# Threshold attention and a MetaFormer block on one core: moving weight conversion earlier, and spreading the ninth slot's transposes

## The chip, the cores and the metric

The kernel runs on one core of one Trainium2 chip. Its engines are TensorE (PE in the profile, with weight loads as PEld), VectorE (DVE), ScalarE (ACT), GpSimd (POOL) and SyncE (SP), which here only issues transfers. The metric is the device time of one execution in microseconds (us). The kernel before takes 1449.51 us, the median of three runs (1449.02 to 1449.96).

## What is computed

Eight batches of eight heads with 576 tokens and a head dimension of 64 go through an attention that keeps only the scores close to the row's maximum. Its result is then read as 576 rows of 512 features per batch, and goes through a layer norm and two dense layers with a residual.

```python
scores = scale * q @ k.T                       # (8, 8, 576, 576)
scores = where(scores >= max - tau, scores, -1e9)
attn   = exp(scores - max); attn /= attn.sum(-1) + 1e-9
x      = (attn @ v) as (8, 576, 512)           # heads side by side
xn     = (x - mean) / sqrt(var + 1e-6) * g_ln
out    = x + relu(xn @ w_ch1) @ w_ch2          # 512 -> 2048 -> 512
```

`w_ch1` and `w_ch2` arrive in 64 bits, and the kernel turns them into 32-bit numbers itself, with integer operations, while the attention of the first batch already runs.

## The kernel before

The work is cut into 72 **slots**, nine for each batch, numbered here as in the code from n = 0 (the "ninth slot" is n = 8, the "tenth" n = 9). In a slot TensorE makes the scores of two heads for one half of the queries; slot 4 of a batch takes what remains of all heads. The values (attention weights times `v`) of a slot are made in the next slot. Each slot has four **quarters**. What was put aside for a quarter is run at its start, and then some **steps** of the dense layers (the second part) follow; a step is one product of 288 columns.

```python
scores(b, s)
run(n, -1)
rest = exponentials(); es, thr = next(rest)      # max, first two exps
run(n, 0)
conversion.fetch(2)                              # weight chunks: issue the transfer
run_all(stores)
second_part(n, 0)
next(rest, None)                                 # the other two exps
...                                              # turn q, k of the next unit; load_qk
run_all(aside)
tick(1); run(n, 1); second_part(n, 1); tick(2)
den = weights(es, thr, blocks_go)                # threshold, sums, reciprocal
if n <= HP or n == 2 * HP:
    diags = diagonals(den)
run_all(aside); run_all(stores)
if HP < n < SLOTS:
    conversion.fetch(2)
tick(3); run(n, 2); second_part(n, 2)
if HP < n < 2 * HP:
    diags = diagonals(den)
tick(4)
...                                              # turn the attention weights, see below
run_all(aside)
conversion.fetch(2)
tick(5); run(n, 3); ...; second_part(n, 3); tick(6)
run_all(aside)
```

**Weight conversion.** There are 32 chunks of 512 KB (64-bit). Sixteen belong to `w_ch1`, sixteen to `w_ch2`. Rooms of a chunk's size are borrowed from tiles that are not yet in use (`hidden`, `et`, parts of `w2`, one of the `x` tiles, and `stage`). `fetch` issues the transfer of a chunk if a room is free for it. A `tick` moves four chunks one stage on: `end` (ACT, only `w_ch1`), `mask` (DVE), `carry` (POOL) and `begin` (two DVE and two ACT operations that read the raw chunk).

```python
def begin(self):
    ...
    nc.vector.tensor_scalar(out=au, in0=hi, ...)           # L263
    nc.vector.scalar_tensor_tensor(out=au, in0=hi, ...)    # L267
    nc.scalar.activation(words(i)[:, :, 0], ..., AF.Copy)  # L271
    nc.scalar.activation(y, words(i)[:, :, 1], AF.Square)  # L275
def carry(self): nc.gpsimd.tensor_tensor(...)              # L281
def mask(self):  nc.vector.scalar_tensor_tensor(...)       # L290
def end(self):   nc.scalar.mul(dst, made, g)               # L303
```

**Turning the attention weights.** In the first batch (n up to 8) TensorE turns them: each of four blocks is multiplied by a diagonal matrix that holds the reciprocal sums (`tp`, copied by ACT into `em`), then the rest (`tr`). From n = 9 on DVE turns blocks of 32 and a trip through DRAM does the rest (`scr<-et`, then `em<-scr`).

```python
made = turn_weights(s, es, diags)        # yields after block 1 and at the end
at_quarter(n + 1, -1, next, made)
at_quarter(n + 1, 0 if s <= HP else -1, ...next(made)...)
at_quarter(n + 1, 1 if b == 0 and s <= HP else 3, ...values_of(b, s, ...)...)
```

In `values_of`, ACT copies the products from `sc[0]` into `x` (L558). From n = 5 on these products lie in a part of the PSUM tile that holds the scores, so the scores of the next slot wait for that copy.

**Second part.** 129 steps for each of 16 groups (half a batch): 64 into `p1` (first layer, relu on ACT into `hidden`), one for the variance, 64 into `p2`. PSUM tiles of this part share two buffers (`ps_ff`) with `tp`, `tr` and `mean`. `second_part` spreads the steps over the slots until the next group is ready; the group after the first is ready at quarter 43 (slot 10, last quarter).

Of the kernel before, what the change touches and what calls it, by code (L numbers as in the profile page):

```python
# [8 lines left out]
F32 = mybir.dt.float32  # L9
# [3 lines left out]
ALU = mybir.AluOpType  # L13
# [5 lines left out]
def kernel(  # L19
# [31 lines left out]
    nc = tc.nc  # L51
# [4 lines left out]
    HP = H // 2  # L56
    NK = DM // 128
    ND = DF // 128
    J = 4
    NB = S // 32  # L60
    TOK = S // 2
    QH = 256
    SLOTS = 2 * HP + 1
    NG = 2 * B
# [9 lines left out]
    ffn = ctx.enter_context(tc.tile_pool(name="ffn", bufs=2))  # L74
# [8 lines left out]
    ident = consts.tile([128, 128], F32, name="ident")  # L83
# [6 lines left out]
    hidden = consts.tile([128, ND, TOK], F32, name="hidden")  # L90
# [53 lines left out]
    for t in rests + v_rest:  # L144
# [9 lines left out]
        out=scl_sb, in0=tau_sb, scalar1=0.0, scalar2=SCALE, op0=ALU.is_ge, op1=ALU.mult  # L154
# [11 lines left out]
    class Weights:  # L166
# [13 lines left out]
        def __init__(self):  # L180
            self.chunks = [
                (w1_sb[i][:, c : c + WC], w_ch1[i * 128 : (i + 1) * 128, c : c + WC], i)
                for c in range(0, DF, WC)
                for i in range(NK)
            ] + [
                (
                    w2_sb[:, m, d : d + 4].rearrange("p d c -> p (d c)"),
                    w_ch2[d * 128 : (d + 4) * 128, m * 128 : (m + 1) * 128].rearrange(
                        "(d p) c -> p d c", p=128
                    ),  # L190
                    None,
                )
                for m in range(NK)
                for d in range(0, ND, 4)
            ]
            self.n1 = NK * (DF // WC)
            self.fetched = self.begun = self.carried = self.masked = self.ended = 0
            self.raw, self.made, self.due, self.ticks = {}, {}, [], 2
            flat = lambda t: t.rearrange("p a b -> p (a b)")

            x_room = ffn.tile([128, NK, TOK], F32, tag="x", bufs=3, name="x_room")
            stage = consts.tile([128, 8, WC], F32, name="stage")
            et = att.tile([128, NB, 128], F32, tag="et", bufs=1, name="et0")

            n1 = self.n1
            self.free = []
            for t, n, before in (  # L210
                (w2_sb.rearrange("p m d c -> p (m d) c"), ND // 2, lambda p: n1 + 2 * p),
                (hidden, 4, lambda p: 8),
                (et, 2, lambda p: 28),
                (x_room, 1, lambda p: 2 * n1),
                (stage, 4, lambda p: 2 * n1),
            ):
                for p in range(n):
                    self.free.append((before(p), -1, flat(t)[:, p * 2 * WC : (p + 1) * 2 * WC]))
# [192 lines left out]
    def weights(es, thr, divide):  # L411


        den = small.tile([128, 4], F32, tag="den", name="den")
        for i in range(4):
            nc.vector.scalar_tensor_tensor(  # L416
                out=es[:, i], in0=blocks[i], scalar=thr[:, i : i + 1], in1=es[:, i],
                op0=ALU.is_ge, op1=ALU.mult, accum_out=den[:, i : i + 1],
            )
        nc.vector.reciprocal(den, den)  # L420
        for i in range(4 if divide else 0):
            nc.gpsimd.tensor_scalar(  # L422
                out=es[:, i], in0=es[:, i], scalar1=den[:, i : i + 1], scalar2=1.0,
                op0=ALU.mult, op1=ALU.mult,
            )
        return den

    def diagonals(den):

        diags = []  # L430
        for i in range(4):
            if i % 2 == 0:
                two = ffn.tile([128, TOK], F32, tag="o", bufs=6, name="diag")
            diags.append(two[:, i % 2 * 128 : i % 2 * 128 + 128])
            nc.scalar.mul(diags[i], ident, den[:, i : i + 1])
        return diags


# [7 lines left out]
    def turn_weights(s, es, diags):  # L446


        em, er = turned_tiles(s)
        for i in range(4):  # L450
            if i == 2:
                yield
            tp = ps_ff.tile([128, J, 128], F32, tag="ff", name="tp")
            for c in range(J):
                product(
                    tp[:, c], lhsT=es[:, i, c * 128 : (c + 1) * 128], rhs=diags[i],
                    start=True, stop=True,
                )
            if s == HP:
                nc.scalar.copy(  # L460
                    em[:, :, :, 32 * i : 32 * i + 32], tp.rearrange("p c (a x) -> p c a x", a=4)
                )
            else:
                h, j = divmod(i, 2)
                nc.scalar.copy(  # L465
                    em[:, :, 2 * j : 2 * j + 2, 64 * h : 64 * h + 64],
                    tp.rearrange("p c (a x) -> p c a x", a=2),
                )
        tr = ps_ff.tile([64, 4, 128], F32, tag="ff", name="tr")
        for i in range(4):  # L470
            nc.tensor.matmul(
                tr[:, i], lhsT=es[:, i, J * 128 :], rhs=diags[i], start=True, stop=True
            )
        if s == HP:
            nc.scalar.copy(
                er[:64].rearrange("p a (u x) -> p u a x", u=HP),
                tr.rearrange("p u (a x) -> p u a x", a=4),
            )
        else:
            nc.scalar.copy(  # L480
                er[:64].rearrange("p a (h x) -> p h a x", h=2),
                tr.rearrange("p (h j) (a x) -> p h (j a) x", h=2, a=2),
            )
        yield em, er
# [112 lines left out]
    def add_to_x(g, m, p2, rb):  # L597
        o = ffn.tile([128, TOK], F32, tag="o", bufs=6, name="o")
        nc.vector.tensor_mul(o, p2, rb)  # L599
        last = (g, m) == (NG - 1, NK - 1)  # L600
        engine = nc.vector if last else nc.gpsimd
        engine.tensor_tensor(out=o, in0=o, in1=groups[g][:, m], op=ALU.add)  # L602
        aside.append(lambda: store(g, m, o))

    def store(g, m, o):
# [4 lines left out]
    def send(g, m, ot):  # L610
        b, t = divmod(g, 2)
        for i in range(4):
            f = m * 128 + 32 * i
            last = (g, m) == (NG - 1, NK - 1)
            (nc.scalar if last and i % 2 else nc.sync).dma_start(
                out=out[b, t * TOK : (t + 1) * TOK, f : f + 32].rearrange(
                    "(n r) c -> r n c", r=32
                ),
                in_=ot[32 * i : 32 * i + 32].rearrange("p (n c) -> p n c", c=32),
            )  # L620
# [17 lines left out]
    def ffn_steps(g):  # L638
# [5 lines left out]
        for d in range(ND):  # L644
# [12 lines left out]
            if d == 1:  # L657
                sq = ffn.tile([128, NK, TOK], F32, tag="sq", bufs=1, name="sq")
                nc.scalar.activation(sq, xc, func=AF.Square)  # L659
                for c in range(1, NK):  # L660
                    nc.gpsimd.tensor_tensor(out=sq[:, 0], in0=sq[:, 0], in1=sq[:, c], op=ALU.add)  # L661
            if d == 8:
                var = ps_ff.tile([128, TOK], F32, tag="ff", name="var")
                product(var, lhsT=avg_sb, rhs=sq[:, 0], start=True, stop=True)
                rb = ffn.tile([128, TOK], F32, tag="rb", bufs=2, name="rb")
                nc.scalar.activation(sq[:, 1], var, func=AF.Identity, bias=eps_sb)
                aside.append(lambda: root(rb, sq[:, 1], sq[:, 2]))
                yield 1
# [19 lines left out]
    ROOM = (0.6, 1.0, 1.25, 0.35)  # L688
    STEPS = 1 + NK * ND * 2
    queue = []  # L690
    issued = 0
    owed = 0.0
    later_calls = {}

    def at_quarter(n, i, fn, *args):
        later_calls.setdefault((n, i), []).append((fn, args))
# [5 lines left out]
    def ready(g):  # L702

        if g < 2:
            return (24, 43)[g]
        b, t = divmod(g, 2)
        return QUARTERS * (b * SLOTS + (HP, 2 * HP)[t] + 2) + (2, 4)[t]

    def second_part(n, i):

        nonlocal issued, owed
        if not queue:
            return
        at = QUARTERS * n + i
# [40 lines left out]
    load_v(1)  # L755
    for n in range(NS):
        b, s = divmod(n, SLOTS)

        ticks = (1, 3) if n < 6 else range(1, 7)

        def tick(i):
            if i in ticks:
# [20 lines left out]
        second_part(n, 1)  # L783
        tick(2)
        blocks_go = by_blocks(b * HP)
        den = weights(es, thr, blocks_go)
        if n <= HP or n == 2 * HP:
            diags = diagonals(den)
        run_all(aside)
        run_all(stores)  # L790
        if HP < n < SLOTS:
            conversion.fetch(2)
        tick(3)
        run(n, 2)
        second_part(n, 2)
        if HP < n < 2 * HP:
            diags = diagonals(den)
        tick(4)
        box = []
        if blocks_go:  # L800
            scr = turn_blocks(s, es)
            at_quarter(n + 1, 0, lambda s=s, scr=scr, box=box: box.append(fetch(s, scr)))
        else:
            made = turn_weights(s, es, diags)
            at_quarter(n + 1, -1, next, made)
            at_quarter(
                n + 1, 0 if s <= HP else -1, lambda made=made, box=box: box.append(next(made))
            )
        at_quarter(
            n + 1, 1 if b == 0 and s <= HP else 3,  # L810
            lambda b=b, s=s, box=box: values_of(b, s, box[0]),
# [51 lines left out]
```

## Time and profile before

| | value |
|---|---|
| time, median of 3 | 1449.51 us |
| span of the profiled run | 1448.2 us |
| TensorE busy | 1392.3 us (96%) |
| VectorE busy | 871.8 us (60%) |
| ScalarE busy | 421.3 us (29%) |
| GpSimd busy | 437.7 us (30%) |
| mean granted TensorE clock | 0.992 |

The profile also shows the span cut into 40 slices of 36.2 us, with each engine's busy share in tenths. Waits are listed as "engine line <- what ended the wait". A busy TensorE is one whose matmuls are pipelined, so its share is not a share of peak. The starts of the slots can be read from the first matmul of line L384 (scores): slot 3 starts at 46.24 us, slot 6 at 81.48, slot 8 at 132.64, slot 9 at 156.74 and slot 10 at 193.26.

### The profile page before, as it was taken

The page shows a single profiled execution, that of the slowest core. Times are in us where ns is not written, and L with a number is a line of the kernel's source. Part 1 is how long each engine was busy: PE and PEld are TensorE (multiplying, and loading weights), DVE is VectorE, ACT ScalarE, POOL GpSimd, SP SyncE. Part 2 cuts the span into 40 slices and gives each one's busy share as a digit, 9 for nine tenths or more (in the row PEclk, how much of TensorE's full clock was granted, in tenths as well). Part 3 has the DMA queues.
Part 4 walks back from the last instruction along what each step waited for, and adds up shares of the span by engine and source line. Part 5 has one row for each costly group of instructions (what it writes and reads, how often), then busy time and mean ns, then how long its engine had stood idle before and what let it go on. Part 6 is the DMA issues. An engine that isn't in the chain of part 4 may idle for free.

```text
span 1448.2 us, 29660 instructions
## 1 busy us (share of the span) xinstructions
PE 1392.3 (96%) x12168; PEld 855.2 (59%) x12168; DVE 871.8 (60%) x1493; ACT 421.3 (29%) x818; POOL 437.7 (30%) x680
## 2 busy tenths in 40 slices
PE   4889869999999999999999999999999999999998
PEld 3666645655556555565556556565655655565565
DVE  5989756566655566656665565656665566655211
ACT  3887313132221313222131222223131222313020
POOL 2344423233323233232333233232332323223100
PEclk8999989999999999999999999999999999999999
DMA  9613366558755677555865577555775568555301
GB/s 226 166 55 101 60 149 159 141 135 165 183 146 144 156 173 154 162 143 134 189 160 149 136 173 167 148 144 143 180 171 141 140 167 174 152 143 136 78 6 17
DMA packets 466840, 205.12 MB, mean 142 GB/s; under 512 B 275024, under 2 KB 428368, under 8 KB 466704
## 3 DMA queue, kind: packets, MB, share of 16 engines
q1 hardware_dynamic: 461328, 202.57, 57.9%
q8 instruction: 95, 1.56, 0.5%
q10 hardware_dynamic: 5344, 0.66, 0.4%
q14 instruction: 41, 0.34, 0.1%
q0 software_dynamic: 32, 0.00, 0.0%
HBM read 119.41 MB, written 83.76 MB: 140 GB/s over the span
## 4 chain that ended last, share of the span: by engine, by line
PE 87%; DVE 7%; ACT 2%; issue 1%; DMA 1%; POOL 1%; SPq 0%; POOLq 0%; ACTq 0%; DVEq 0%
PE p L100 64%; PE sc L384 10%; PE sc L541 10%; DVE e L416 2%; DVE neg L398 1%; PE tp L100 1%; ACT e L409 1%; DVE w L290 1%; PE mean L100 1%; DVE w L263 0%; DMA em<-scr 0%; DMA stage<-in_moe_w_ch_dram 0%; POOL e L422 0%; PE var L100 0%; ACT em L465 0%
## 5 line engine op out<-in xcount | busy, mean ns | idle before, releaser
L100 PE MATMUL p<-xc,w 128*64 128x288 f32 x4096 | 515.9, 408 | 8.0 <-ACT hidden L655 7.4
L100 PE MATMUL p<-hidden,w 128*64 128x288 f32 x4096 | 513.9, 407 | 0.0
L100 PEld LDWEIGHTS p<-xc,w 128*64 128x64 f32 x4096 | 292.3, 137 | 216.2 <-ACT hidden L655 17.2
L100 PEld LDWEIGHTS p<-hidden,w 128*64 128x64 f32 x4096 | 295.3, 137 | 199.6 <-issue 9.7
L398 DVE TENSOR_REDUCE neg<-sc 128x2 f32<-128x1152 f32 x144 | 188.8, 1353 | 254.2 <-PE sc L384 254.2
L409 ACT ACTIVATE e<-sc,neg 128x576 f32<-128x576 f32 x288 | 194.4, 741 | 259.6 <-DVE neg L398 259.6
L422 POOL TENSOR_SCALAR e<-e,den 128x576 f32<-128x576 f32 x252 | 188.2, 764 | 232.2 <-DVE den L420 232.2
L416 DVE SCALAR_TENSOR_TENSOR e<-sc,thr,e 128x576 f32<-128x576 f32 x288 | 219.3, 812 | 20.5 <-ACT e L409 20.5
L497 DVE STREAM_TRANSPOSE et<-e 128x1152 f32<-128x1152 f32 x112 | 153.3, 1374 | 77.2 <-POOL e L422 54.1
L655 ACT ACTIVATE hidden<-p 128x288 f32<-128x288 f32 x256 | 105.5, 412 | 275.7 <-PE p L100 274.0
L384 PE MATMUL sc<-kT,qT 64*128 64x384 f32 (+3 forms) x1024 | 154.0, 433 | 32.5 <-ACT x L558 12.4
L384 PEld LDWEIGHTS sc<-kT,qT 64*128 64x128 f32 x1024 | 96.2, 194 | 91.0 <-issue 27.8
L402 POOL TENSOR_SCALAR thr<-neg,low_sb 128x2 f32<-128x2 f32 x144 | 41.5, 288 | 356.2 <-DVE neg L398 350.3
L541 PE MATMUL sc<-em,v_in 128*64 128x256 f32 (+1 forms) x1408 | 130.8, 329 | 0.6 <-DMA em<-scr 0.4
L558 ACT COPY x<-sc 128x256 f32<-128x256 f32 x60 | 22.3, 372 | 316.9 <-PE sc L541 293.7
L541 PEld LDWEIGHTS sc<-em,v_in 128*64 128x64 f32 x1408 | 86.1, 137 | 39.3 <-DVE et L497 1.5
L602 POOL TENSOR_TENSOR o<-o,x 128x288 f32<-128x288 f32 x63 | 50.6, 803 | 149.3 <-DVE o L599 149.3
L599 DVE TENSOR_TENSOR o<-p,rb 128x288 f32<-128x288 f32 x64 | 28.1, 439 | 106.4 <-PE p L100 105.8
L567 POOL TENSOR_TENSOR sum<-sum,x 128x256 f32<-128x256 f32 (+1 forms) x64 | 32.4, 506 | 80.8 <-ACT x L558 78.2
L661 POOL TENSOR_TENSOR sq<-sq 128x288 f32<-128x288 f32 x48 | 38.7, 807 | 43.7 <-ACT sq L659 41.2
L567 POOL TENSOR_TENSOR sum<-x 128x256 f32<-128x256 f32 (+1 forms) x32 | 16.8, 525 | 102.8 <-ACT x L558 59.1
L541 PE MATMUL sc<-rest,v_rest 128*64 128x256 f32 (+1 forms) x352 | 44.3, 329 | 0.0
(133 smaller groups left out, 717.9 us busy)
## 6 DMA issues: line engine op xcount, KB each, us to landing
scr<-et SPq DMA_DIRECT2D x252, 288.0 KB, 4.6
em<-scr SPq DMA_DIRECT2D x63, 1024.0 KB, 5.9
out_dram<-ot SPq DMA_DIRECT2D x254, 36.0 KB, 4.2
q_in<-in_q_dram SPq DMA_DIRECT2D x124, 72.0 KB, 3.2
k_in<-in_k_dram SPq DMA_DIRECT2D x120, 72.0 KB, 2.8
v_in<-in_v_dram SPq DMA_DIRECT2D x64, 128.0 KB, 4.4
rest<-scr SPq DMA_DIRECT2D x63, 128.0 KB, 5.9
w<-in_moe_w_ch_dram SPq DMA_DIRECT2D x11, 512.0 KB, 5.4
```

What stands on the lines that cost most here:

```text
L100: nc.tensor.matmul(out[r], lhsT=lhsT[:, r], rhs=rhs, **flags)
L384: nc.tensor.matmul(sc[h][64 * i : 64 * i + 64 if s == HP else 128, at : at + n], lhsT=ql[r] if s == HP else qT[r, half, j * 128 : (j + 1) ...
L398: nc.vector.tensor_reduce(out=neg[:, i], in_=pairs[h], axis=AXL.X, op=ALU.max, negate=True,)
L402: nc.gpsimd.tensor_scalar(out=thr[:, i], in0=neg[:, i], scalar1=-1.0, scalar2=low_sb, op0=ALU.mult, op1=ALU.add,)
L409: nc.scalar.activation(es[:, i], blocks[i], func=AF.Exp, bias=neg[:, i : i + 1])
L416: nc.vector.scalar_tensor_tensor(out=es[:, i], in0=blocks[i], scalar=thr[:, i : i + 1], in1=es[:, i], op0=ALU.is_ge, op1=ALU.mult, accum_o ...
L422: nc.gpsimd.tensor_scalar(out=es[:, i], in0=es[:, i], scalar1=den[:, i : i + 1], scalar2=1.0, op0=ALU.mult, op1=ALU.mult,)
L497: nc.vector.transpose(et[:, :, 64 * h : 64 * h + 64].rearrange("p n (j c) -> p j n c", j=2), es[:, 2 * h : 2 * h + 2].rearrange("p j (n c) ...
L541: nc.tensor.matmul(dst[64 * h : 64 * h + 64], lhsT=vt[:, c, h, :] if c < J else vr[:, h, :], rhs=pick(em[:, c] if c < J else er, hp, h), s ...
L567: nc.gpsimd.tensor_tensor(out=sums[g][:, cols], in0=x[:, 0, cols] if c == 1 else sums[g][:, cols], in1=x[:, c, cols], op=ALU.add,)
L602: engine.tensor_tensor(out=o, in0=o, in1=groups[g][:, m], op=ALU.add)
L655: nc.scalar.activation(hidden[:, d], p1, func=AF.Relu)
```

## The change

It moves the conversion of the weights forward: slots 3 to 5 get a third tick. The extra `fetch` in the middle of slots 5 to 8 is gone, and two kinds of rooms may be borrowed for longer (`hidden` up to chunk 10, `et` up to chunk 32). The diagonals are always made right behind the reciprocal. The four blocks of the ninth slot are turned in four places of the tenth slot (before the quarters, and in quarters 0, 1 and 2) in place of all at its start. The second group of the dense layers is ready one quarter earlier. The variance's product is not made in a slot's first quarter (unless the first layer ends there). The very last addition goes to GpSimd like all others, and the last four stores are all issued by SyncE.

```diff
-                (hidden, 4, lambda p: 8),
-                (et, 2, lambda p: 28),
+                (hidden, 4, lambda p: 10),
+                (et, 2, lambda p: 2 * n1),
... weights(): the diagonals are made here, behind the reciprocal
-    def diagonals(den):
+            if not divide:
+                ...
+                nc.scalar.mul(diags[i], ident, den[:, i : i + 1])
+                continue
... turn_weights()
-            if i == 2:
+            if i:
                 yield
... add_to_x(), send()
-        last = (g, m) == (NG - 1, NK - 1)
-        engine = nc.vector if last else nc.gpsimd
-        engine.tensor_tensor(out=o, in0=o, in1=groups[g][:, m], op=ALU.add)
+        nc.gpsimd.tensor_tensor(out=o, in0=o, in1=groups[g][:, m], op=ALU.add)
-            (nc.scalar if last and i % 2 else nc.sync).dma_start(
+            nc.sync.dma_start(
... ffn_steps()
-            if d == 8:
+            if d >= 8 and rb is None and (part or d == ND - 1):
... ready()
-            return (24, 43)[g]
+            return (24, 42)[g]
... the loop over slots
-        ticks = (1, 3) if n < 6 else range(1, 7)
+        ticks = (1, 3, 4)[: 2 + n // 3] if n < 6 else range(1, 7)
-        if HP < n < SLOTS:
-            conversion.fetch(2)
-            at_quarter(n + 1, -1, next, made)
-            at_quarter(
-                n + 1, 0 if s <= HP else -1, lambda made=made, box=box: box.append(next(made))
-            )
+            for i, at in enumerate(
+                (-1, -1, 0, 0) if s <= HP else (-1, -1, -1, -1) if s < 2 * HP else (-1, 0, 1, 2)
+            ):
+                if i < 3:
+                    at_quarter(n + 1, at, next, made)
+                else:
+                    at_quarter(n + 1, at, lambda made=made, box=box: box.append(next(made)))
```

More of the change, by code (lines that the diff above doesn't have):

```diff
@@ L420, in weights @@
         nc.vector.reciprocal(den, den)
-        for i in range(4 if divide else 0):
+        diags = []
+        for i in range(4):
+            if not divide:
+                if i % 2 == 0:
+                    two = ffn.tile([128, TOK], F32, tag="o", bufs=6, name="diag")
+                diags.append(two[:, i % 2 * 128 : i % 2 * 128 + 128])
+                nc.scalar.mul(diags[i], ident, den[:, i : i + 1])
+                continue
             nc.gpsimd.tensor_scalar(
@@ L425, in weights @@
             )
-        return den
-    def diagonals(den):
[L430 to L435, printed above, removed]
         return diags
@@ L613, in send @@
             f = m * 128 + 32 * i
-            last = (g, m) == (NG - 1, NK - 1)
-            (nc.scalar if last and i % 2 else nc.sync).dma_start(
+            nc.sync.dma_start(
                 out=out[b, t * TOK : (t + 1) * TOK, f : f + 32].rearrange(
@@ L690 @@
     queue = []
-    issued = 0
+    issued = part = 0
     owed = 0.0
@@ L709, in second_part @@
     def second_part(n, i):
-        nonlocal issued, owed
+        nonlocal issued, owed, part
+        part = i
         if not queue:
@@ L785 @@
         blocks_go = by_blocks(b * HP)
-        den = weights(es, thr, blocks_go)
-        if n <= HP or n == 2 * HP:
-            diags = diagonals(den)
+        diags = weights(es, thr, blocks_go)
         run_all(aside)
         run_all(stores)
-        if HP < n < SLOTS:
-            conversion.fetch(2)
         tick(3)
@@ L795 @@
         second_part(n, 2)
-        if HP < n < 2 * HP:
-            diags = diagonals(den)
         tick(4)
```

## The prediction

> **What bounds the kernel now.** I read the page's slices first. They show where TensorE is not full.
>
> ```profile
> PE   4889869999999999999999999999999999999998
> DVE  5989756566655566656665565656665566655211
> PEclk8999989999999999999999999999999999999999
> ```
>
> From slice 8 on (253 us) TensorE stands at 9: nothing but fewer matmuls helps there, and the change removes none. The loss lies in the first seven slices, with VectorE at 9 in slices 3 and 4, and in the sixth, where the clock dips too. So I cut this stretch by slots, at the starts of the score matmuls (from, width, then busy us with counts for PE, PEld, DVE, ACT, POOL, then clock, DMA share and GB/s):
>
> ```profile
> 46.24:57.89 11.65, 10.09 (x109) 7.86 (x109) 11.55 (x18) 10.52 (x22) 5.03 (x5) 1.00 0.94 225
> 57.89:69.66 11.77, 9.99 (x124) 7.47 (x124) 11.67 (x18) 10.41 (x21) 4.83 (x5) 1.00 0.29 92
> 69.66:81.48 11.82, 10.41 (x168) 8.62 (x168) 11.72 (x18) 10.39 (x21) 4.83 (x5) 1.00 0.02 3
> 81.48:109.77 28.29, 24.51 (x228) 15.58 (x224) 22.31 (x37) 22.89 (x47) 14.90 (x17) 1.00 0.28 82
> 109.77:132.64 22.87, 21.36 (x211) 14.14 (x209) 22.46 (x35) 18.25 (x37) 9.63 (x8) 1.00 0.49 144
> 132.64:156.74 24.10, 21.59 (x212) 14.41 (x212) 23.36 (x39) 15.23 (x30) 9.73 (x10) 1.00 0.28 59
> 156.74:193.26 36.52, 24.01 (x212) 19.71 (x212) 18.94 (x31) 8.12 (x14) 11.86 (x13) 0.88 0.40 90
> 193.26:216.41 23.15, 21.20 (x154) 13.41 (x154) 17.34 (x30) 4.24 (x7) 9.67 (x12) 0.89 0.51 117
> ```
>
> These are slots 3 to 10. In slots 3 to 5 VectorE is busy 99% of the time: it bounds them. Slot 9 takes 36.52 us for as many matmuls (212) as slot 8 runs in 24.10. Its waits name the cause; the timelines of PE, ACT and SP show it:
>
> ```profile
> 193.26 4.21 PE L384 MATMUL sc<-kT,qT 64*128 64x384 f32 x16 [9.77 <-ACT x L558]
> 191.70 0.68 ACT L271 ACTIVATE stage<-stage 128x512 int32<-128x512 uint32 x1 [18.66 <-DMA stage<-in_moe_w_ch_dram]
> 192.83 0.38 ACT L558 COPY x<-sc 128x256 f32<-128x256 f32 x1
> 181.33 4.20 SPq L503 DMA_DIRECT2D scr<-et  x4
> 185.63 2.86 SPq L243 DMA_DIRECT2D stage<-in_moe_w_ch_dram  x2
> ```
>
> Slot 10's scores wait 9.77 us for a copy of 0.38 us. The copy stands on ACT behind a `begin` whose chunk was fetched in the same quarter. That fetch stood on SP behind slot 9's four `scr` writes.
>
> **What the Trainium skill says.** "TensorE: Matmul & The Clock Gate", on the array's architecture, says that the ACT and DVE queues are strictly first in, first out. The trace agrees: the copy starts at 192.83, straight behind the two `begin` operations, though its product was ready about 10 us earlier. Part 1 of that page says that an idle TensorE falls to a slower clock. Here the granted clock is 0.88 in slot 9, and the scores after the gap take 4.21 us where those at 216.34 take 2.21. "SBUF — State Buffer", on who interferes with whom, says that some DVE operations and GpSimd exclude each other on a shared port pair. The trace fits: L263 takes 0.41 us, but 1.52 us in cases where a `carry` runs beside it.
>
> **The change part by part.** I stepped through the code's counters (fetch, tick, rooms, steps owed) for both versions; for the kernel before they give the order of transfers and steps in the trace.
>
> *Step unit.* The chain has "PE p L100 x100" in 12.28 us; a step is four such records, 0.49 us. A slot without turning blocks needs 2.14 (scores) + 2.16 (values), with turning 3.73 (`tp`) + 0.90 (`tr`) more: 8.9 us beside the steps.
>
> *Third tick, slots 3 to 5.* The counters put the last three fetches (chunks 29, 30, 31) at the ends of slot 8 (29, 30) and the start of slot 9 (31), where before 29 came at the start and 30, 31 at the end of slot 9. A tick costs VectorE a mask, L263 and L267: from the groups of 46 to 82 us 0.85 + 0.88 + 1.43 = 3.2 us, about 2.7 back to back. VectorE has no gap in slots 3 and 4: 2 x 2.7 = **+5.4 us** on the end of slot 5. The third one, in slot 5, comes behind what slot 6's scores wait for, and slot 6 has gaps on VectorE: +0.5.
>
> *More steps early.* With its group ready a quarter earlier, the pacing puts 32, 25, 29, 29, 30 steps in slots 6 to 10 (before: 28, 25, 26, 26, 28), and 129 in slots 11 to 15 (before 141). The sum is the same; what counts is whether the 12 moved steps (5.9 us) fall in gaps. Slot 6: 28.29 us now, 23.3 of it needed; four more steps +1.5. Slot 7: no change of steps. Slot 8: needs 14.2 + 8.9 = 23.1, and I allow 1.0 for waits: 24.1, as before.
>
> *Diagonals earlier, slots 5 to 7.* ACT then waits for `den` ahead of the relus of quarter 2. In slot 7 `den` is there at 123.5 while PE reaches that quarter at about 122; with two `p1` buffers I put +0.7 on this.
>
> *The stall itself.* In slot 8 nothing is written to `scr` (TensorE turns there), so SP reaches chunk 29 behind the q and k loads: 143.93 + 4.1 us, 15.4 us into the slot. These chunks took 6.0 us to land at this stage (median between 140 and 220 us), so 21.8 us into the slot. ACT comes free at 20.4 (diagonals end at 153.07). The `begin` (1.1) and the copy would end near 23.4, while PE has work until 23.1. So the stall shrinks from 9.77 us to below 1, and chunk 31 lands long before slot 9's first tick.
>
> *Blocks of the ninth slot spread.* PE's waits on ACT in slot 9 are 3 x 0.7 before `tp` and 0.7 before `tr`. Between steps the copies have time, so 2.1 go; the last stays, since `tr` still follows the fourth block. A new wait of about 1.3 is likely: the fourth block needs the buffer of a `p2` that VectorE reads only behind slot 9's thresholds. Slot 9: 14.2 + 8.9 = 23.1 needed, + 2.9 for waits = **26.0, before 36.52**.
>
> *Slot 10.* 30 steps 14.7 + mean 0.6 + 4.3 = 19.6, + 0.6 for a wait = 20.2, before 23.15 (cold scores and a wait of 1.95 for `mean`). *Slots 11 to 15*: -12 steps = -5.9, and -0.7 for the variance of the second group, whose product moves from slot 12's second quarter to slot 11's last. Later groups of the kernel before make it in quarters 1 or 2 already, so four waits of 0.70 stay.
>
> *Tail.* The last addition: 0.80 + handoffs on POOL (1427.67 to 1429.04, 1.37 us from product to transpose) for 0.99 on DVE: +0.4. Four issues on SP take 1.83, two on each of two engines 0.89: +0.9.
>
> | part | us |
> |---|---|
> | third ticks (5.4 + 0.5) | +5.9 |
> | slot 6, steps | +1.5 |
> | slot 7, diagonals | +0.7 |
> | slot 8 | 0.0 |
> | slot 9 (26.0 - 36.5) | -10.5 |
> | slot 10 (20.2 - 23.15) | -3.0 |
> | slots 11 to 15 | -6.6 |
> | tail | +1.3 |
> | sum | -10.7 |
>
> 1449.5 - 10.7 = 1438.8; I say **1438.5 us**.
>
> **The rivals.** *The stall only moves.* Chunk 29 is begun by the tick that follows its fetch, as chunk 30 was before. If SP is late in slot 8, or the q and k loads (small packets, just ahead of it) slow the transfer, ACT blocks there, up to 5 us, with a cold clock behind it. For it: the same code pattern. Against it: no `scr` writes ahead, and a full slot of PE work. It would make 1443 to 1447. *VectorE pays it all.* But for slot 6 (79%), slots 3 to 8 run VectorE at 97 to 99%; if the third ticks collide with `carry` each time (3.2 us) and slots 6 to 8 pass every delay on, about +5 more: 1444. *The early slots swallow the ticks.* The same chunks then leave slots 8 and 9, where VectorE was late (slot 8 at 97%); if slots 7 and 8 also become shorter, -4 more: 1434. *PE was full anyway*, so that only the gap counts: gains of slot 9 alone less the ticks, 1444.
>
> **Range and chances.** The rivals lie between 1434 and 1447, the sum at 1438.8. 1431 to 1447 should hold it 8 times in 10. Over 2% faster would be below 1420.5, which is 18 us beyond the sum; over 2% slower, above 1478.5, would need a stall larger than any in the trace. So faster 0.02, same 0.97, slower 0.01.
>
> **What would show it.** Slots 3 and 4 last 14.3 us; slot 6 starts near 87, slot 9 near 165, slot 10 near 191, slot 11 near 211. The wait of scores for ACT's copy is below 2 us everywhere. The chunk fetches of slot 8 are issued about 15 us into it. No `tp` wait of 0.7 comes three in a row in slot 9. The last DMA issue ends 1.3 us later behind the last matmul. I am wrong if VectorE passes less or more than 2.7 us a tick on to slot 6, or if slot 8's copy waits for a transfer.

## The result, and the profile after

The changed kernel takes 1440.17 us (median of six runs, 1438.01 to 1441.93). Six runs of the kernel before, taken beside them, have a median of 1450.35 us. The ratio is 0.9923, with a 95% interval of 0.9903 to 0.9943: 0.8% faster. Predicted were 1438.5 us, between 1431 and 1447, and "within 2%".

First the slices of the page after. Slice 5 no longer shows an 8, and the 6 in slice 6 has become a 9; slice 3 has gone from 8 to 7. The dip of the clock there is gone as well.

```profile
PE   4879999999999999999999999999999999999998
DVE  5997957556665666566665565656665666655111
PEclk8999999999999999999999999999999999999999
```

Now slots 3 to 10, cut as for the kernel before (from, width, then busy us with counts for PE, PEld, DVE, ACT, POOL; clock, DMA share, GB/s):

```profile
46.38:57.60 11.22, 10.05 (x109) 7.86 (x109) 11.12 (x18) 9.22 (x19) 4.37 (x5) 1.00 0.93 210
57.60:72.06 14.46, 10.13 (x125) 7.47 (x124) 14.32 (x21) 12.31 (x25) 6.36 (x6) 1.00 0.42 137
72.06:86.66 14.60, 10.54 (x168) 8.62 (x168) 14.46 (x21) 11.96 (x24) 6.37 (x6) 1.00 0.22 71
86.66:120.81 34.15, 28.14 (x244) 17.40 (x241) 26.36 (x44) 25.12 (x51) 18.72 (x19) 0.95 0.26 81
120.81:143.09 22.28, 21.63 (x211) 13.95 (x209) 19.62 (x30) 16.41 (x33) 8.82 (x8) 1.00 0.25 72
143.09:166.04 22.95, 22.95 (x227) 15.35 (x225) 22.24 (x38) 14.05 (x27) 9.21 (x10) 1.00 0.44 98
166.04:190.73 24.69, 23.32 (x227) 17.86 (x225) 16.93 (x28) 7.08 (x13) 10.95 (x13) 1.00 0.43 89
190.73:211.18 20.45, 19.70 (x162) 11.58 (x161) 12.59 (x24) 5.30 (x9) 7.80 (x12) 1.00 0.63 144
```

Slot 9 fell from 36.52 to 24.69 us with 15 more matmuls in it. Slots 4 and 5 are 2.7 and 2.8 us longer, with VectorE at 99% as before, and slot 6 is 5.9 us longer. The timelines of SP, ACT and PE at the end of slot 8 show what became of the chunk that used to stall:

```profile
159.01 0.44 SPq L243 DMA_DIRECT2D w<-in_moe_w_ch_dram  x1
163.29 0.70 ACT L271 ACTIVATE w<-w 128x512 int32<-128x512 uint32 x1 [0.59 <-DMA w<-in_moe_w_ch_dram]
164.45 0.39 ACT L555 COPY x<-sc 128x256 f32<-128x256 f32 x1
166.04 2.21 PE L384 MATMUL sc<-kT,qT 64*128 64x384 f32 x16
```

Chunk 29 is issued 15.9 us into slot 8, and ACT waits 0.59 us for it. The copy then starts 1.6 us before the scores, which have no wait. The same ordering hazard is in the code, but TensorE has work over it.

### The profile page after: what moved, and what is told of

The parts are those of the page before. It is cut to its first block, busy times and chain, and to the rows that moved or that the text cites. A ratio compares the mean times of both kernels' runs of the same rounds, so it can differ in the third digit from the quotient of the medians.

```text
span 1438.0 us, 29661 instructions
## 1 busy us (share of the span) xinstructions
PE 1389.3 (97%) x12168; PEld 851.0 (59%) x12168; DVE 868.9 (60%) x1492; ACT 421.7 (29%) x818; POOL 439.0 (31%) x681
## 4 chain that ended last, share of the span: by engine, by line
PE 89%; DVE 5%; ACT 2%; DMA 2%; issue 1%; SPq 1%; POOL 0%; POOLq 0%; DVEq 0%; ACTq 0%
PE p L100 67%; PE sc L538 10%; PE sc L384 10%; DVE e L416 1%; PE tp L100 1%; DMA v_in<-in_v_dram 1%; DVE neg L398 1%; SPq L115 1%; ACT e L409 1%; PE mean L100 0%; DVE et L494 0%; DVE w L263 0%; PE var L100 0%; DMA qk_room<-in_q_dram 0%; ACT hidden L649 0%
## 5 line engine op out<-in xcount | busy, mean ns | idle before, releaser
L384 PE MATMUL sc<-kT,qT 64*128 64x384 f32 (+3 forms) x1024 | 150.0, 424 | 20.9 <-DVE e L416 10.8
```

The source lines that it names most:

```text
L384: nc.tensor.matmul(sc[h][64 * i : 64 * i + 64 if s == HP else 128, at : at + n], lhsT=ql[r] if s == HP else qT[r, half, j * 128 : (j + 1) ...
```

## The experiments

Theory 1: the gain is the stall of slot 9 that goes, since the last chunks are issued ahead of slot 9's `scr` writes; the third ticks and the early diagonals are its price. The rivals were that earlier steps, spread blocks or early conversion as such carry it. "At slot 16" below means the start of slot 16's scores; from there on TensorE is the bound in all these kernels, and they differ by single waits. From slot 16 to slot 71 the traces take between 1021.4 and 1026.1 us (the changed kernel 1022.6, and 1023.8 in its second trace, run 9). Slot starts already differ by up to 1 us at slot 3 between runs of the same kernel. Both limit what such a difference can tell.

**1. The stall alone.** The kernel before, with one more fetch:

```diff
         second_part(n, 1)
         tick(2)
+        if n == SLOTS:                  # slot 9
+            conversion.fetch(2)
```

> The kernel before with one more fetch of two chunks in slot 9, behind its second tick, so that chunks 30 and 31 are issued ahead of slot 9's scr writes. Nothing else of the change. Theory 1 (the change's gain is the stall in slot 9 that goes, less what the third ticks cost): the 9.8 us wait of slot 10's scores for ACT's copy falls below 1 us, slot 9 lasts 25 to 27 us (36.5 before), slot 10 about 21, and the kernel takes 1436 to 1439, ratio 0.990 to 0.993, as good as the changed one without any third tick. Theory 2 (the gain comes from the 12 steps that are done earlier, and from the spread blocks): 1446 or more, since neither is in it.

Measured: 1440.88 us, ratio 0.9911 (0.9878 to 0.9944), against the changed kernel's 0.9923. On SP the two chunks now stand ahead of the `scr` writes, and slot 10's scores start at once:

```profile
169.65 1.80 SPq L243 DMA_DIRECT2D stage<-in_moe_w_ch_dram  x2
183.51 3.81 SPq L503 DMA_DIRECT2D scr<-et  x4
...
183.81 2.21 PE L384 MATMUL sc<-kT,qT 64*128 64x384 f32 x16
```

Slot 9 lasts 26.68 us and slot 16 starts 10.1 us earlier than before. This one fetch gives the whole gain of the change, so theory 1 stands. The ratio is in the range that I expected. The time is 2 to 5 us above it, but the kernel before, measured beside it, took 1453.5 us here. Slot 10 lasted 22.46 us in place of about 21, because the mean still waited 2.03 us for VectorE.

**2. The third tick alone.** The kernel before with `ticks = (1, 3, 4)[: 2 + n // 3]`.

> The kernel before with only the third tick in slots 3 to 5. By the counters chunk 31 is still fetched at the end of slot 9, behind the scr writes, and begun at once. Theory 1: the stall stays at 7 to 10 us, slot 6 starts 5.2 us later, and the kernel gets slower: 1452 to 1456. Rival (converting earlier is what gains, whatever the last fetch does): 1440 to 1444.

Measured: 1451.96 us, ratio 0.9994 (0.9982 to 1.0005): neither slower nor faster. The stall is there as theory 1 says, 7.50 us:

```profile
186.17 1.60 SPq L243 DMA_DIRECT2D stage<-in_moe_w_ch_dram  x1
192.70 0.67 ACT L271 ACTIVATE stage<-stage 128x512 int32<-128x512 uint32 x1 [17.57 <-DMA stage<-in_moe_w_ch_dram]
...
194.27 4.21 PE L384 MATMUL sc<-kT,qT 64*128 64x384 f32 x16 [7.50 <-ACT x L558]
```

But the price came back: slot 6 starts 6.4 us later than before (0.6 of that is there at slot 2 already), and slot 16 only 0.8 later. Slots 7 and 8 are 0.65 and 1.44 us shorter, slot 9 3.9. The scores at the start of slot 9 waited 2.52 us for ACT's copy in the kernel before, and ran slowly behind that:

```profile
156.74 3.73 PE L384 MATMUL sc<-kT,qT 64*128 64x384 f32 x16 [2.52 <-ACT x L558]
```

Here they wait 0.94 us and take 2.21. Of slot 9's 3.9 us, 2.3 are the shorter stall and 1.5 these scores. So I had booked the ticks as pure cost, and most of it comes back as shorter waits later.

**3. The diagonals.** The changed kernel with the diagonals of slots 5 to 7 behind the steps of quarter 2, as before.

> The changed kernel with the diagonals of slots 5 to 7 made where they were before, behind the steps of quarter 2. Slot 6 lasts 34.15 us in the changed kernel, 28.29 before; PE waits 2.77 us there for a relu behind the diagonals, and its matmuls then come at 0.24 us in place of 0.12 for about 3.5 us. Theory 1 (the diagonals are the cause of both): that wait falls to about 1.6, no slow stretch behind it, slot 6 lasts 31 to 31.5, the kernel 1437 to 1438. Rival (the four more steps and the third tick of slot 5 are the cause): slot 6 stays above 33, the kernel at 1440.

Measured: 1438.10 us, ratio 0.9898 (0.9873 to 0.9923), slot 6 at 30.86 us. PE's timeline in slot 6 of the changed kernel:

```profile
106.06 2.16 PE L100 MATMUL p<-xc,w 128*64 128x288 f32 x16 [1.01 <-ACT hidden L649]
110.99 4.18 PE L100 MATMUL p<-xc,w 128*64 128x288 f32 x20 [2.77 <-ACT hidden L649]
```

and with late diagonals:

```profile
106.38 2.16 PE L100 MATMUL p<-xc,w 128*64 128x288 f32 x16 [1.00 <-ACT hidden L652]
110.16 2.65 PE L100 MATMUL p<-xc,w 128*64 128x288 f32 x20 [1.61 <-ACT hidden L652]
```

The wait is 1.2 us shorter, the length of the four diagonals on ACT, and the same 20 matmuls behind it take 2.65 us in place of 4.18. Slot 6 is 3.3 us shorter: 1.2 from the wait, 1.7 from the slow matmuls behind it (1.5 here, 0.2 in the values), 0.4 from a shorter wait of `tp`. Half pace behind this wait is not certain, though: of the five traces in which it lasts 2.76 or 2.77 us, four show it, and run 7 does not (last section).

**4. Two ticks and the extra fetch, in the changed kernel.**

> The changed kernel with two ticks in slots 3 to 5 as before, and the extra fetch of the first run in slot 9. The rest of the change stays. Theory 1: the third ticks are pure cost once the last chunks are fetched ahead of the scr writes; slot 6 starts 5 us earlier than in the changed kernel, slot 9's stall stays away, and the kernel takes 1434 to 1437. Rival (earlier conversion relieves VectorE in slots 7 to 9 by as much as it costs): 1439 to 1441.

With two ticks the rooms in `hidden`, kept to chunk 10 here, are overwritten by relus before one chunk has left them, so one weight chunk is not what it should be; the operations and their order are the same as otherwise. Measured: 1440.81 us, ratio 0.9927. Slot 6 starts 5.6 us earlier, but slot 9 lasts 31.03 us, 6.3 more than in the changed kernel, because the fourth block waits 3.28 us for a buffer that VectorE has to read, and the matmuls behind it run at half pace for a while. By time the rival is right. Run 11 repeats it with sound rooms.

**5. The ninth slot's blocks at the start.** The changed kernel with `(-1, -1, -1, -1)` for all slots above the fourth.

> The changed kernel with all four blocks of the ninth slot turned at the start of slot 9, as before. Slot 9 lasts 24.69 us in the changed kernel, with two waits of 0.7 for ACT's copies. Theory 1 (spreading saves what the waits show): two more waits of 0.7, slot 9 at 26.0 to 26.5, the kernel 1441 to 1442. Rival (the title's change is what removes the stall): the wait of slot 10's scores returns, slot 9 above 30, 1446 or more.

Measured: 1441.69 us, ratio 0.9936 (0.9919 to 0.9954); slot 9 lasts 26.50 us, with all four waits of about 0.7 for ACT's copies. Slot 16 starts 1.5 us later. Spreading these blocks is worth 1.5 to 1.8 us here and has nothing to do with the stall.

**6. The second group ready at quarter 43.**

> The changed kernel with the second group ready at quarter 43 as before, so that slots 6 to 10 get 133 steps in place of 145. Theory 1 (the moved steps fall in few gaps): slot 6 lasts 32 to 33 us in place of 34.15, slots 11 to 15 are 6 us longer together, the wait of the mean for VectorE in slot 10 (1.95 us before) returns; at slot 16 the difference to the changed kernel is +1 to +3 us. Rival (the earlier steps are a main part of the gain): +6 us.

Measured: 1443.51 us, ratio 0.9948 (0.9931 to 0.9965). Slot 6 lasts 32.20 us. At slot 10 this kernel is 5.1 us ahead of the changed one, and at slot 16 0.2 behind (0.5 ahead at slot 6 already, so 0.7 lost): the moved steps are paid where they go, and the small rest is the mean's wait, 1.44 us, and one of 0.70 for a relu in slot 12. Against the trace of run 9, where the changed kernel has no long wait in slot 12, 1.7 us are lost. At slot 71 this kernel is 3.15 us behind. Behind slot 16 it has four waits of 0.70, in the places where the kernel before has them, and the changed kernel has one: 2.1 us. The rest are waits of the values for transfers, which differ from run to run. One of the four in its PE timeline:

```profile
396.88 8.47 PE L100 MATMUL p<-xc,w 128*64 128x288 f32 x68 [0.70 <-ACT hidden L649]
```

**7. The variance as before** (`if d == 8`).

> The changed kernel with the variance's product always behind the ninth block of the first layer, as before. By the counters it moves only for the last group (slot 75, after the attention has ended). Expected: slot starts up to slot 71 within 0.5 us of the changed kernel's up to what runs differ by (0.6 us in the first three slots), time 1438 to 1442. Rival (the variance's place carries part of the gain): waits of PE for ACT's relu of 0.7 us come back in several groups, 3 us or more in the sum.

Measured: 1439.33 us in one run; slot 71 starts 0.4 us earlier than in the changed kernel, and no wait came back. (Slot 6 starts 1.1 us later, ahead of anything that the edit touches.) The variance's rule does nothing that can be seen here. The four waits belong to the ready quarter of run 6: the rounding of steps owed is carried on from group to group, and with 42 in place of 43 the first quarter of slot 21 gets eight steps in place of four (32 matmuls in place of 16 between slot 21's scores and the variance's product in the two traces). The relu that was late in run 6 stands on ACT between the slot's exponentials.

**8. Late diagonals and the old tail**, in the changed kernel.

> The changed kernel with the diagonals of slots 5 to 7 at their old place and the last addition and the last stores as before (VectorE; SyncE and ScalarE in turn). Expected from its parts: the late diagonals took the span from 1438.0 to 1436.6, and the tail behind the last matmul is 6.3 us in the changed kernel, 5.05 before: 1.2 less, a span of 1435 to 1436 and 1436 to 1437.5 us, ratio 0.988 to 0.990; faster than both kernels. Rival (the tail is hidden by the last transfer anyway): no change against the run with late diagonals alone, 1438.

Measured: 1433.82 us, ratio 0.9890 (0.9871 to 0.9909), span 1431.8. The tail behind the last matmul is 5.1 us again, 1.1 less than the changed kernel's 6.2 with GpSimd and SyncE alone. That is what the old tail can give. The medians of runs 3 and 8 lie 4.3 us apart, but they were not taken side by side; their ratios differ by 0.0008, which is 1.2 us. Their operations are the same up to the tail, and yet at slot 71 this profile is 3.7 us ahead of run 3's.

**9 and 10. The changed kernel and that of run 8, side by side.**

> The changed kernel as it is, to stand beside the next run on the same chip. Expected: 1438 to 1441 us, ratio 0.991 to 0.994, slot starts within 1 us of its first profile.

> The kernel of the eighth run once more (changed kernel, diagonals of slots 5 to 7 late, old tail), beside the changed one on the same chip. Expected: 4 to 6 us below it (3.3 from slot 6, 1.2 from the tail), 1433 to 1436 us. Rival (the 1433.8 was a good draw): less than 3 us below.

Measured: 1439.28 us (1437.65 to 1440.60; ratio 0.9911, 0.9895 to 0.9927) and 1436.62 us (1433.46 to 1438.60; 0.9893, 0.9875 to 0.9911). The medians lie 2.7 us apart, which is what the rival said (less than 3). In the traces slot 16 starts 2.7 us earlier and slot 71 5.0, and the spans are 1437.8 and 1431.7; but the second trace is of the fastest of its five runs. So the version is faster than the kernel before; it was below the changed kernel both times, but by how much is left open by the spread of the runs.

**11. Two ticks, the extra fetch, and the rooms to chunk 8**, in the kernel of run 8.

> That kernel with two ticks in slots 3 to 5 as before, the extra fetch in slot 9, and the hidden rooms kept to chunk 8 (the fourth run kept them longer, so one weight chunk was overwritten there). Theory 1 (third ticks are a price of 5 us): slot 6 starts 5.2 us earlier and most of it stays: 1429 to 1431. Theory 3 (VectorE's work is only moved: what slots 4 and 5 lose, slots 7 to 9 gain): slot 6 starts 5.2 us earlier, slots 7 to 9 are 4 to 6 us longer together, with VectorE late in slot 9 and a wait of the fourth block for a buffer that VectorE reads, and the time is 1433 to 1436.

Measured: 1436.26 us, ratio 0.9892 (0.9874 to 0.9909), the same as run 10. Slot 6 starts 5.7 us earlier, slot 10 0.9 later than in run 10. The lead goes in slot 9, which lasts 31.30 us in place of 24.69; slots 7 and 8 took only 0.6 of it. PE's timeline there:

```profile
173.53 1.98 PE L100 MATMUL tp<-diag,e 128*64 128x128 f32 x16 [3.57 <-DVE o L599]
176.19 1.75 PE L471 MATMUL tr<-diag,e 128*64 128x128 f32 x7 [0.69 <-ACT em L465]
```

Without the third ticks VectorE has conversions left in slot 9, reads `p2` late, and the fourth block waits for that buffer; the matmuls behind that wait run at half pace. Theory 3 is right in the sum (the time is just above its range) and theory 1's account of the ticks is wrong: with the blocks spread, they buy back in slot 9 what they cost in slots 4 and 5. Whether they would with the blocks at the start stays open. Run 1 has two ticks and its blocks there, and its slot 9 lasts 26.68 us with three steps fewer; that would leave about 3 us of the lead (an estimate from these two slots), and no run combines it with the rest of run 11.

## Why the prediction was right, point by point

| step | predicted | measured |
|---|---|---|
| start of slot 6 | +5.4 | +5.2 |
| slot 6 | +2.0 | +5.9 |
| slot 7 | +0.7 | -0.6 |
| slot 8 | 0.0 | -1.2 |
| slot 9 | -10.5 | -11.8 |
| slot 10 | -3.0 | -2.6 |
| slots 11 to 15 | -6.6 | -5.5 |
| slot 16 to the last matmul | 0 | -0.7 |
| tail | +1.3 | +1.2 |
| sum (span) | -10.7 | -10.2 |

- **The stall** was read rightly: it went, and the remaining wait of ACT for the transfer was 0.59 us. Run 1 shows that nothing else is needed for it. The rival that it would only move did not come true. By the prediction's own sign, "if slot 8's copy waits for a transfer", it was not quite right: the copy stood behind that `begin`, only too briefly to matter. The 15.4 and 6.0 us that it adds up make 21.4, not 21.8; the `begin` started 20.2 us into the slot.
- **The third ticks** cost 5.2 us ahead of slot 6, at the rate I had taken from the groups. I put them one slot too early: the scores of slot 4 come ahead of slot 3's third tick on VectorE, so slots 4 and 5 grew, not 3 and 4. And the sum has no line for what they relieve later. The third rival, that slots 7 and 8 become shorter, was partly true: they became 1.7 us shorter where I had 0.7 longer. In slot 7 a wait of 1.35 us for a relu is gone, and one of 0.63 for another operation of ACT came. In slot 8 the wait of 2.52 us at its end, which the sum does not name, is gone, against three more steps (1.5). (VectorE stands at 9 in slices 2 and 4 of the page before, and at 8 in slice 3; the prediction has slices 3 and 4.)
- **Slot 6** is the term that was mis-sized. I put 0.5 for the tick, 1.5 for the steps, and the diagonals' price on slot 7. In the traces the 5.9 us are: four more steps 2.0; `tp` waiting 1.0 longer for ACT, 0.6 of it by the third tick of slot 5 (run 2 has this alone) and 0.4 by the diagonals; the relu waiting 1.2 longer behind the diagonals; and 1.7 of half pace behind that wait (1.5 in the 20 matmuls, 0.2 in the values). Run 3 takes the last two away, with 0.4 of the `tp` wait, and gets 3.3 us. In slot 7 the diagonals cost nothing that I can see.
- **Slot 9** came out 1.3 us better than the sum, because the fourth block did not wait for `p2`. Of the 2.9 us for waits the prediction names 0.7 and 1.3; measured are two of 0.69 and 0.68. Runs 4 and 11 show that this wait is real, and larger than I put it, once VectorE is later.
- **The four waits of 0.70** did not stay: after 300 us PE waits for a relu once. The step that failed is "later groups make it in quarters 1 or 2 already": the quarter was right, but not the number of steps ahead of it in the slot. Runs 6 and 7 put this on the ready quarter. In the trace after, 1.8 us of other waits (values for VectorE, at 739 and 907 us) stand against it.
- **Slots 11 to 15** gave 5.5 us in this profile, with a wait of 0.82 us for VectorE in slot 12. In run 9's profile of the same kernel they give the predicted 6.6.
- **Moved steps** are worth 0.7 to 1.7 us up to slot 16 by run 6: paid where they go for the most part.

In short, the main mechanism was right: the stall goes, and the third ticks cost about 5 us ahead of slot 6. That the total came out within 2 us is luck: slot 6 was too low by 3.9 and slots 7 to 9 too high by 3.8.

## What to carry to other kernels

Look at what stands ahead of a transfer in its issuing queue, not only at when the code asks for it: one fetch moved ahead of a write that waits for late data was worth 10 us here, and the rest of the change about nothing. An in-order engine (ACT here) that first reads a fresh transfer and then frees a buffer hands that transfer's latency on to everyone who waits for the buffer. A cost on a busy engine is not a loss until one has looked at where the same work would have stood otherwise.

## What the runs showed of the hardware

A wait of TensorE can cost more than itself: behind some waits the matmuls run at half pace for a while. Take the second wait for a relu in slot 6. Where it lasts 1.59 to 1.61 us (seven traces: the kernel before, runs 1 to 3, 8, 10 and 11), the matmuls behind it keep their pace. Where it lasts 2.76 or 2.77 us, they fall to half of it in four traces of five (the changed kernel, runs 5, 6 and 9). Behind the waits of 3.28 and 3.57 us in slot 9 (runs 4 and 11) 16 `tp` matmuls took 1.98 us in place of 1.09. Behind the wait of 2.77 in the changed kernel the matmuls came every 0.24 us in place of 0.12, for some 3.5 us, and the clock in the profile's window from 113 to 116 us is 0.61:

```profile
113.00:116.00 3.00, 3.00 (x18) 1.64 (x16) 2.93 (x6) 1.74 (x4) 0.06 (x2) 0.61 0.04 10
```

The fifth trace is that of run 7, whose operations up to there are the same. The same 20 matmuls behind the same wait take 2.65 us there in place of 4.18, and a `tp` wait 19 us earlier has half pace behind it instead (in the changed kernel that one lasts 1.77 us, and the 48 matmuls take 2.87):

```profile
93.53 4.51 PE L100 MATMUL tp<-diag,e 128*64 128x128 f32 x48 [1.92 <-ACT em L462]
112.63 2.65 PE L100 MATMUL p<-xc,w 128*64 128x288 f32 x20 [2.76 <-ACT hidden L649]
```

So the length of the wait alone does not decide. Waits of 2.03 and 2.00 us (run 1 at 195 us, run 11 at 906 us) also had half pace behind them, and one of 1.95 (the kernel before, at 207 us) had not. What decides between about 1.9 and 2.8 us is not shown.

The Trainium skill, "TensorE: Matmul & The Clock Gate", Part 1, gives an idle window of about 3.4 us for the fall to the slower clock. Here waits of about 2 us were enough at times, and one of 2.76 us was not.
